# Two chained gated layers behind a linear attention: the last down product of block 0 from halves, blocks 1 and 2 sent out through partial rows in DRAM, and a new order of the first 400 tasks

## The chip, the cores and the metric

One NeuronCore of a Trainium2 chip runs the whole program. The metric is device time in microseconds (us), the median over runs. TensorE (PE in the rows) multiplies, VectorE (DVE) and ScalarE (ACT) do elementwise work, GpSimd (POOL) issues the accumulating transfers and SyncE (SP) all other transfers.

## What is computed

```python
def _attn_ref(q, k, v):                      # batch 2, 8 heads, 768 steps, head size 64
    for t in range(S):
        state = gamma * state + einsum('bhd,bhe->bhde', k[:, :, t], v[:, :, t])
        y[:, :, t] = scale * einsum('bhd,bhde->bhe', q[:, :, t], state)

def _moe_ref(x, w_in, w_out):                # 1536 tokens, 512 -> 2048 -> 512
    h = x @ w_in
    return (h * clip(h + 3, 0, 6) / 6) @ w_out

def _moe2_ref(x, w_in, w_out):               # the same sizes
    h = x @ w_in
    return (h * tanh(log1p(exp(h)))) @ w_out

x = attention output as (1536, 512);  out = _moe2_ref(_moe_ref(x))
```

All in float32. The kernel keeps that precision by splitting each operand of a big product into a high and a low part and multiplying three times (high by high, low by high, high by low).

## The kernel before

The 1536 tokens are three blocks (0, 1, 2) of 512 columns. The 2048 hidden rows are 16 tiles of 128, taken as eight pairs `p`, and the pairs as four groups `g` of two (`NG = 4`, `NP = 2`). In every layer a group first makes its hidden tiles (up products) and then multiplies them by the second weight matrix (down products), so there are eight rounds of up and down, after an attention part.

Blocks 1 and 2 of a pair are, but for one pair of the first group, made together by a scheme with seven products instead of eight (`up_pair`, products `P1` to `P7`, who = "w"; block 0 is done the same way with halves of its own columns, who = "v"). Six matmuls make one product. Its recombination runs through three PSUM tiles X, Z (tags `wx`, `wy`) and Y (`wy`): `s1` copies X to SBUF on ScalarE (L930), product 2 goes into Y, and `c11` adds Y to the copy on VectorE (L933). The activation then reads the sum.

The down products of a group of the second layer are one of three (the first layer has `pair_down` in groups 1 and 2, and direct products else):

- `pair_down` ("p"): blocks 1 and 2 together, seven products `k` in the order 1, 5, 6, 3, 7, 2, 4 of twelve matmuls of 512 columns each.
- `half_down` ("b" of the groups in `HD`, before 1 and 2): block 0 by the same seven products, but on two halves of 256 columns; twelve matmuls of 256 columns to a product. Ahead of each, VectorE forms a difference (`less`, L1204), ScalarE rounds to the high part (L1225) and VectorE makes the low part (L1226).
- `block_down` ("b" of the others): block 0 directly, four tiles by four output rows by three matmuls of 512 columns.

`AFTER` says the order in a group: ("bp", "bp", "bp", "pb"), so the last group does `pair_down` first and block 0 last. What a group adds to the output is copied out of PSUM (`copied`, L1057, ScalarE) and added to partial rows in DRAM (`into_part`: the first write by SP, L1069, the later ones by an accumulating transfer of POOL, L1071). In the last group nothing goes to the partial rows: `read_back` (L1080) brings all of them to SBUF, `into_back` adds the products onto them on VectorE (L1063) and SP stores the sums to the output (L1098).

The order of all work is made when the program is built: each step is a task with an engine, a modelled duration and its dependencies; the first tasks stand in the string `SEQ`, word for word in the order in which they are issued, and the rest is put in order by rank and modelled time (`Plan.order`). Each engine then runs its own tasks strictly in that order, SP's transfers too. In the names of tasks `lq`, `lk` and `w0_` are loads of queries with keys, of values, and of weights; `sc`, `kv`, `qv`, `pv` are the attention products of one of twelve units; `hi`, `lo` make the parts of a hidden tile; `y` is a store to the output. `TOPS` and `KPD` say by a letter which engine (A for ScalarE, D for VectorE) does one conversion of a weight load, or one scaling of values.

Of the kernel before, what the change touches and what calls it, by code (L numbers as in the profile page):

```python
# [70 lines left out]
HD = (1, 2)  # L71
# [4 lines left out]
SEQ = ("ones cst0 lq0 dum0 zero lq1 dum1 tri top0 dum2 rows dum3 lk0 dum4 lk1 warm0 lk2 warm1 lq2 sc0 lq3 lq4 sc1 m0_0 m0_1 tab0 "  # L76
# [18 lines left out]
BORDER = {"pb": (2, 3, 0, 1), "bp": (0, 1, 2, 3)}  # L95
TOPS = "AAAAAAADDADADDAAAAAADDAAAADDAAAA"
KPD = "DDDDDDAAADAA"
# [154 lines left out]
def body(ctx: ExitStack, tc: tile.TileContext, aps: dict, out: bass.AP):  # L252
# [640 lines left out]
    def up_pair(who, layer, p):  # L893
# [10 lines left out]
        n = first.stop  # L904

# [34 lines left out]
        s1 = snap(1, X, first, g11, first, p1)  # L940
        if seq_of(who, layer, p) == EARLY_Y:
            p2 = product(2, Y, True, first, [p1])
            p5 = product(5, Z, True, last, [p2])
        else:
            p5 = product(5, Z, True, last, [p1])
            p2 = product(2, Y, True, first, [p5])
# [415 lines left out]
    for g in range(NG):  # L1362
        for key in flow1[g]:
            need(key)
        if g == NG - 1:
            for b in (1, 2, 0):
                read_back(b)
# [74 lines left out]
```

## Time and profile before

| | |
|---|---|
| runs | median 530.24 us of 3 (529.26 to 533.11) |
| profiled execution, its own time | 528.86 us |
| its span in the trace | 527.1 us |
| TensorE busy | 521.0 us (99%) |
| VectorE busy | 447.2 us (85%) |
| ScalarE busy | 356.0 us (68%) |
| GpSimd busy | 58.0 us (11%) |
| mean granted clock of TensorE | 0.998 of full speed |

The span runs from the first to the last instruction; the profiled execution's own time is 1.76 us more. Matmuls overlap in the trace (one of 512 columns is shown with 390 ns, though the next one starts after about 227 ns), so their pace is read from a run of many, not from the mean of one.

### The profile page before, as it was taken

Reading aid. Unit: us, or ns where it says so; the run is one execution under the profiler, and the core shown is the slowest. Engines: PE = TensorE matmul, PEld = TensorE weight load, DVE = VectorE, ACT = ScalarE, POOL = GpSimd, SP = SyncE. Lnnn points to the kernel's source line nnn. Section 1 sums busy time; section 2 is a strip of 40 time slices with the busy share of each in tenths; the row PEclk is TensorE's granted clock in tenths of the full one; section 3 lists DMA queues with packets and bytes.
Section 4 is the critical chain, followed back from the end, with each engine's and each line's share of the span. In section 5 each row is a group of like instructions: output and inputs, shape, how many; then the busy total and the mean of one; then the engine's idle time right before and its main releaser. Section 6 shows DMA issues by size and latency. Waiting matters only on the chain.

```text
span 527.1 us, 8602 instructions
## 1 busy us (share of the span) xinstructions
PE 521.0 (99%) x3186; PEld 444.7 (84%) x3186; DVE 447.2 (85%) x745; ACT 356.0 (68%) x646; POOL 58.0 (11%) x70
## 2 busy tenths in 40 slices
PE   8999999999999999999999999999999999999996
PEld 5888888888889888888888898888998899888885
DVE  4999998799998969778889999977899879987892
ACT  3488496757786666686655777776768778786540
POOL 1000000001330020340000000020024300540000
PEclk9999999999999999999999999999999999999999
DMA  8995115443994362798530024682149941995532
GB/s 329 406 410 196 29 52 168 159 156 92 175 193 124 134 139 35 147 127 267 195 130 2 0 81 140 220 199 100 63 116 150 241 133 32 183 123 116 188 137 105
DMA packets 27179, 78.92 MB, mean 150 GB/s; under 512 B 3024, under 2 KB 4432, under 8 KB 27136
## 3 DMA queue, kind: packets, MB, share of 16 engines
q1 hardware_dynamic: 17920, 61.58, 32.3%
q0 software_dynamic: 9216, 16.78, 22.1%
q8 instruction: 25, 0.41, 0.3%
q14 instruction: 18, 0.15, 0.1%
HBM read 52.13 MB, written 26.21 MB: 149 GB/s over the span
## 4 chain that ended last, share of the span: by engine, by line
PE 97%; DMA 1%; DVE 1%; issue 0%; DVEq 0%
PE acc L285 50%; PE wx L285 26%; PE wy L285 21%; DMA kv<-in_kv_dram 1%; DVE A L687 0%; DVE vp L680 0%; DVE xch L1063 0%; DVEq L1437 0%; DVE t L494 0%; DVE bias L266 0%; DVEq L680 0%
## 5 line engine op out<-in xcount | busy, mean ns | idle before, releaser
L285 PE MATMUL acc<-gh,wdl 128*128 128x512 f32 (+1 forms) x216 | 82.6, 382 | 0.0
L285 PE MATMUL acc<-gh,wdh 128*128 128x512 f32 (+1 forms) x216 | 82.5, 382 | 0.0
L285 PE MATMUL acc<-gl,wdh 128*128 128x512 f32 (+1 forms) x216 | 82.3, 381 | 0.0
L1071 POOL DMA_DIRECT2D part<-sb x42 | 37.6, 937 | 387.9 <-ACT sb L1057 294.5
L285 PE MATMUL acc<-gh,sb 128*128 128x512 f32 (+1 forms) x204 | 57.1, 365 | 0.0
L285 PEld LDWEIGHTS acc<-gl,wdh 128*128 128x128 f32 x216 | 40.6, 188 | 7.9
L612 DVE TENSOR_TENSOR cv<-cv 128x256 f32<-128x256 f32 x108 | 45.5, 422 | 1.6
L285 PEld LDWEIGHTS acc<-gh,wdh 128*128 128x128 f32 x216 | 40.7, 188 | 7.2
L285 PEld LDWEIGHTS acc<-gh,wdl 128*128 128x128 f32 x216 | 40.7, 188 | 7.1
L979 ACT CAST gh<-g 128x512 fp32r<-128x512 f32 x54 | 33.5, 621 | 18.0 <-PE acc L285 13.7
L981 DVE TENSOR_TENSOR gl<-g,gh 128x512 fp32r<-128x512 f32 x54 | 37.2, 688 | 9.8 <-PE acc L285 4.8
L285 PEld LDWEIGHTS acc<-gh,sb 128*128 128x128 f32 x204 | 36.5, 189 | 5.9
L554 DVE SCALAR_TENSOR_TENSOR cv<-raw,top 128x1024 int32<-128x1024 int32 (+1 forms) x34 | 39.3, 1157 | 0.4 <-ACT top L549 0.2
L285 PE MATMUL acc<-gl,sb 128*128 128x512 f32 (+1 forms) x102 | 37.1, 364 | 0.0
L979 ACT CAST gh<-gs 128x512 fp32r<-128x512 f32 x43 | 26.7, 620 | 14.9 <-PE acc L285 14.1
L1057 ACT ACTIVATE sb<-acc 128x512 f32<-128x512 f32 x52 | 30.9, 600 | 6.5 <-PE acc L285 5.7
L549 ACT ACTIVATE top<-raw 128x1024 f16<-128x1024 bf16 (+1 forms) x25 | 32.1, 1283 | 1.1 <-DMA raw<-in_w_dram 1.1
L981 DVE TENSOR_TENSOR gl<-gs,gh 128x512 fp32r<-128x512 f32 x43 | 29.6, 688 | 3.4 <-ACT gh L979 2.8
L565 DVE SCALAR_TENSOR_TENSOR wdl<-cv,wdh 128x512 fp32r<-128x512 f32 x32 | 21.6, 686 | 7.6 <-ACT wdh L563 7.3
L285 PE MATMUL wy<-xbh,wsh 128*128 128x512 f32 x60 | 23.5, 392 | 0.0
L285 PE MATMUL wy<-xbh,wsl 128*128 128x512 f32 x60 | 23.4, 390 | 0.0
L285 PE MATMUL wx<-q,wsh 128*128 128x512 f32 x60 | 23.3, 389 | 0.0
(252 smaller groups left out, 1459.0 us busy)
## 6 DMA issues: line engine op xcount, KB each, us to landing
raw<-in_w_dram SPq DMA_DIRECT2D x30, 1023.8 KB, 4.8
part<-sb POOLq DMA_DIRECT2D x42, 256.0 KB, 5.0
qk<-in_qk_dram SPq DMA_DIRECT2D x12, 512.0 KB, 7.3
kv<-in_kv_dram SPq DMA_DIRECT2D x10, 516.0 KB, 6.4
part<-sb SPq DMA_DIRECT2D x18, 256.0 KB, 2.1
part<-q POOLq DMA_DIRECT2D x10, 256.0 KB, 4.9
q<-part SPq DMA_DIRECT2D x8, 256.0 KB, 6.1
raw<-in_w_dram SPq DMA_DIRECT2D x4, 511.8 KB, 7.9
```

Of the source, the lines that this page charges most:

```text
L285: nc.tensor.matmul(o, l, r, start=start, stop=stop, skip_group_check=True)
L549: a1 = add(nm + "t", "ACT", act(n) * 1.33, [ld, top_free[0]], [rb, t_b], lambda: A.activation(top(), high(), AF.Copy, scale=0.5))
L554: top_free[0] = add(nm + "o", "DVE", dve(n), [a1], [rb, t_b, cb], lambda: V.scalar_tensor_tensor(out=cb.tile.bitcast(I32)[:, cs], in0=low( ...
L565: return add(nm + "lo", "DVE", dve(n), [a], list(dict.fromkeys([cb, hb, lb])), lambda: V.scalar_tensor_tensor(out=lb.tile[:, l0:l0 + n], i ...
L612: prev = [add(nm + f"s{o}", "DVE", dve(256), prev, [cb], lambda o=o, x=x, y=y, op=op: V.tensor_tensor(out=q(o), in0=q(x), in1=q(y), op=op))]
L979: a = add(f"hi{nm}", "ACT", act(512), deps + [prev_split[0]], [gb, gh], lambda: A.copy(gh.tile, gb.tile))
L981: lambda: V.tensor_tensor(out=gl.tile, in0=gb.tile, in1=f32(gh.tile), op=ALU.subtract))
L1057: lambda: A.activation(tp.tile, ac.tile, AF.Copy, scale=sc), rk)
L1071: landed[tp] = added[layer, b, d] = add(f"pa{nm}", "POOL", ADDED, [dep, added[layer, b, d], *more], [tp, pt], lambda: nc.gpsimd.dma_start( ...
```

## The change

Three edits that can be told apart, and a table.

1. `HD` gets group 3: the last block-0 product is `half_down` in place of `block_down`. Its sums are added onto the rows read back and stored in eight pieces of 256 columns.
2. `pair_down` of the last group no longer uses `into_back`: its products are copied out by ScalarE and accumulated into the partial rows by POOL, as in the other groups, and once a row has had its last addition SP copies it from the partial row to the output, DRAM to DRAM (new, L1196 of the changed kernel). Only block 0's rows are read back (four transfers in place of twelve).
3. `ONTO` lists eight pairs for which `s1` copies X into the PSUM tile Y instead of SBUF; product 2 is then accumulated onto it (no fresh start), the addition `c11` is gone, and the activation reads Y.
4. `SEQ` has another order and more tasks, and `TOPS`, `KPD` change three letters each.

```diff
+ONTO = ((0, 2), (0, 3), (0, 5), (0, 6), (0, 7), (1, 3), (1, 5), (1, 7))
-HD = (1, 2)
+HD = (1, 2, 3)
...
-    "m1_0 otab0 tab1 otab1 tab4 m1_1 tab2 vp0 tab5 tab3 otab5 vp1 kv0 otab3 pv0 lk3 kv1 vp2 pv1 st1 lk4 otab4 lq5 st0 xf1_0 "
+    "otab2 m0_1 tab4 tab0 vp0 tab1 otab0 m1_1 otab1 kv0 pv0 lk3 vp1 tab5 tab3 otab5 vp2 kv1 st0 otab4 pv1 lk4 otab3 lq5 kv2 "
...
-TOPS = "AAAAAAADDADADDAAAAAADDAAAADDAAAA"
-KPD = "DDDDDDAAADAA"
+TOPS = "AAAAADDADADADDAAAAAADDAAAADDAAAA"
+KPD = "DDDDAAADADAA"
...
+        early = seq_of(who, layer, p) == EARLY_Y
+        onto = who == "w" and not early and ((layer, p) in ONTO)
...
-        s1 = snap(1, X, first, g11, first, p1)
+        s1 = snap(1, X, first, Y if onto else g11, first, p1)
...
-            p2 = product(2, Y, True, first, [p5])
+            p2 = product(2, Y, not onto, first, [p5] + ([s1] if onto else []))
...
-        c11 = plus(11, Y, first, g11, first, [p2, s1])
+        c11 = p2 if onto else plus(11, Y, first, g11, first, [p2, s1])
...
-            gval[layer, f, 1] = (g11, [mish_or_swish(f"{layer}_{f}_1", layer, g11, [c11])])
+            gval[layer, f, 1] = (g11, [mish_or_swish(f"{layer}_{f}_1", layer, g11, [c11], src=Y if onto else None)])
...
-                if final:
-                    into_back(nm, ac, b, dd, [last[d]], rk, k in (3, 7, 2, 4))
-                    ev[banks[k][d]] = back[b, dd][1] if k not in (3, 7, 2, 4) else []
-                elif k == 3:
+                if k == 3:
...
+                if layer and g == NG - 1 and k in (3, 7, 2, 4):
+                    pt = part[1, b, dd]
+                    add(f"y{nm}", "SP", 0.8, [added[1, b, dd]], [pt], lambda b=b, dd=dd, pt=pt: nc.sync.dma_start(
+                        out=out[dd * P:(dd + 1) * P, b * TB:(b + 1) * TB], in_=pt.tile))
...
-            for b in (1, 2, 0):
-                read_back(b)
+            read_back(0)
```

On SP, at the very end of the program, this stands before; `xal`, `xah` and `xch` are the rows of blocks 2, 1 and 0 in SBUF:

```order
L1098 DMA out_dram<-xal_5152 128x512 x4
L1098 DMA out_dram<-xah_5149 128x512 x4
L1098 DMA out_dram<-xch_5243 128x512 x3
L1098 DMA out_dram<-xch_5243 128x256 x2
L1437 UNCONDITIONAL_BRANCH
```

and this after the change; `part_337` to `part_340` are block 1's partial rows, `part_341` to `part_344` block 2's:

```order
L1196 DMA out_dram<-part_341_3614 128x512
L1196 DMA out_dram<-part_342_3621 128x512
L1196 DMA out_dram<-part_343_3546 128x512
L1279 DMA out_dram<-xch_5232 128x256 x2
L1196 DMA out_dram<-part_337_3514 128x512
L1279 DMA out_dram<-xch_5232 128x256 x4
L1196 DMA out_dram<-part_344_3554 128x512
L1279 DMA out_dram<-xch_5232 128x256 x2
L1196 DMA out_dram<-part_338_3524 128x512
L1196 DMA out_dram<-part_339_3694 128x512
L1196 DMA out_dram<-part_340_3698 128x512
L1445 UNCONDITIONAL_BRANCH
```

The stores of block 0 were the last of the queue; now three copies of partial rows stand behind the last two of them.

On TensorE block 0 came last before, tile by tile; near its end stood

```order
L285 MATMUL acc_987_5417<-wbl_995_5441,wdh_5091 128x512
L285 MATMUL acc_984_5424<-wbh_994_5436,wdh_5091 128x512
L285 MATMUL acc_984_5424<-wbh_994_5436,wdl_5103 128x512
L285 MATMUL acc_984_5424<-wbl_995_5441,wdh_5091 128x512
L285 MATMUL acc_985_5429<-wbh_994_5436,wdh_5091 128x256
```

and now, as far from the end, stands the seventh half product, whose matmuls read `wbh_1000` and `wbl_1001`, the parts that ScalarE and VectorE make:

```order
L288 MATMUL acc_997_5531<-gl_5502,wdh_5084 128x256
L288 MATMUL acc_982_5409<-wbh_1000_5519,wdh_4984 128x256
L288 MATMUL acc_982_5409<-wbh_1000_5519,wdl_4994 128x256
L288 MATMUL acc_982_5409<-wbl_1001_5535,wdh_4984 128x256
L288 MATMUL acc_983_5422<-wbh_1000_5519,wdh_4984 128x256
```

All 84 matmuls behind the last pair product have 256 columns, where 45 of 512 and 6 of 256 stood.

On SP near the start, the eleventh to sixteenth transfer (`kv` values, `qk` queries with keys, `raw` weights) stood before as

```order
L315 DMA kv_177<-in_kv_dram 128x1032
L315 DMA kv_199<-in_kv_dram 128x1032
L303 DMA qk_219<-in_qk_dram 128x1024
L534 DMA raw_237<-in_w_dram 128x2047
L315 DMA kv_261<-in_kv_dram 128x1032
```

and now as

```order
L318 DMA kv_171<-in_kv_dram 128x1032
L318 DMA kv_193<-in_kv_dram 128x1032
L306 DMA qk_217<-in_qk_dram 128x1024
L318 DMA kv_237<-in_kv_dram 128x1032
L537 DMA raw_258<-in_w_dram 128x2047
```

The first three, and all ahead of them, keep their places; the weights are one place later.

## Rows read from the trace of the kernel before

**Rows 1.** The page's first part: busy time, share and instructions of each engine
```profile
span 527.1 us, 8602 instructions
PE 521.0 (99%) x3186; PEld 444.7 (84%) x3186; DVE 447.2 (85%) x745; ACT 356.0 (68%) x646; POOL 58.0 (11%) x70
```

**Rows 2.** Busy time by stretch; last columns: granted clock, DMA share, GB/s
```profile
core 0: us, PE busy (x) PEld busy (x) DVE busy (x) ACT busy (x) POOL busy (x), PEclk, DMA share, GB/s
4.32:20.00 15.68, 15.08 (x255) 12.62 (x256) 11.26 (x18) 5.87 (x13) 0.00 (x0) 1.00 1.01 392
...
20.00:60.00 40.00, 39.89 (x540) 34.25 (x537) 38.06 (x64) 28.74 (x76) 0.00 (x0) 1.00 0.68 264
...
500.00:520.00 20.00, 20.00 (x90) 16.57 (x89) 13.84 (x23) 6.53 (x11) 0.00 (x0) 1.00 0.29 107
```

**Rows 3.** All that TensorE waited for: us in total, times, longest
```profile
PE acc L285 <- DVE t L494: 1.2, 1, 1.2
PE acc L285 <- DVE vp L680: 0.3, 1, 0.3
PE wy L285 <- DVE A L687: 0.2, 1, 0.2
```

**Rows 4.** The chain that ended last, from 10 us: start, us, what
```profile
10.30 6.43 DMA kv<-in_kv_dram
...
17.57 2.03 PE acc L285 x48
```

**Rows 5.** The same chain later: runs of down products and one up product
```profile
390.28 1.39 PE wx L285 x6
391.67 19.04 PE acc L285 x84
...
436.62 5.03 PE acc L285 x42
...
495.05 27.95 PE acc L285 x126
```

**Rows 6.** Line 930, the copies out of PSUM: ns min/median/max, first and last start
```profile
L930 ACT COPY gs<-wx x15: 569/587/590, 82.7 to 483.2; 128x512 f32<-128x512 f32 x15
```

**Rows 7.** VectorE in order of time during a half product: start, us, what
```profile
435.65 0.42 DVE L1204 TENSOR_TENSOR wsl<-wsl 128x256 f32<-128x256 f32 x1
435.99 0.42 DVE L1204 TENSOR_TENSOR wsh<-wsh 128x256 f32<-128x256 f32 x1
...
438.33 0.42 DVE L1226 TENSOR_TENSOR wbl<-wsl,wbh 128x256 fp32r<-128x256 f32 x1
...
439.74 0.42 DVE L1226 TENSOR_TENSOR gl<-wsl,gh 128x256 fp32r<-128x256 f32 x1 [0.15 <-ACT gh L1225]
```

**Rows 8.** All engines in order of time: the pair product's last split, and the end
```profile
508.46 0.69 DVE L981 TENSOR_TENSOR gl<-gs,gh 128x512 fp32r<-128x512 f32 x1 [0.23 <-PE acc L285]
...
522.71 0.28 PE L285 MATMUL acc<-wbl,wdh 128*128 128x256 f32 x1
...
523.02 0.76 DVE L1063 TENSOR_TENSOR xch<-acc,xch 128x256 f32<-128x256 f32 x2
523.03 1.33 SPq L1098 DMA_DIRECT2D out_dram<-xch  x3
```

**Rows 9.** SP's issues in order of time: three in a row
```profile
493.60 1.37 SPq L1080 DMA_DIRECT2D xch<-part  x3
```

**Rows 10.** Transfers from 520 us on: KB each, median us from issue to landing
```profile
out_dram<-xch SPq DMA_DIRECT2D x3, 256.0 KB, 2.4
out_dram<-xch SPq DMA_DIRECT2D x2, 128.0 KB, 2.1
```

**Rows 11.** SP's twelve reads of partial rows, 484 to 495 us
```profile
DMA to landing us min/median/max: 2.6/3.9/5.0
```

**Rows 12.** The page's DMA issues: reads of the first layer's partial rows
```profile
q<-part SPq DMA_DIRECT2D x8, 256.0 KB, 6.1
```

**Rows 13.** POOL's accumulating transfers of the third group, 440 to 480 us
```profile
DMA to landing us min/median/max: 3.8/4.7/6.5
```

**Rows 14.** The page's groups: issue of an accumulating transfer, copy out of PSUM
```profile
L1071 POOL DMA_DIRECT2D part<-sb x42 | 37.6, 937 | 387.9 <-ACT sb L1057 294.5
L1057 ACT ACTIVATE sb<-acc 128x512 f32<-128x512 f32 x52 | 30.9, 600 | 6.5 <-PE acc L285 5.7
```

More of the change, by code (lines that the diff above doesn't have):

```diff
@@ L75 @@
 AFTER = ("bp", "bp", "bp", "pb")
-SEQ = ("ones cst0 lq0 dum0 zero lq1 dum1 tri top0 dum2 rows dum3 lk0 dum4 lk1 warm0 lk2 warm1 lq2 sc0 lq3 lq4 sc1 m0_0 m0_1 tab0 "
[18 rows of a table removed]
+SEQ = ("ones cst0 lq0 dum0 zero lq1 dum1 tri top0 dum2 rows dum3 lk0 dum4 lk1 warm1 lk2 warm0 lq2 sc0 lq3 lq4 sc1 m0_0 tab2 m1_0 "
[20 rows of a table added]
 BORDER = {"pb": (2, 3, 0, 1), "bp": (0, 1, 2, 3)}
-TOPS = "AAAAAAADDADADDAAAAAADDAAAADDAAAA"
-KPD = "DDDDDDAAADAA"
+TOPS = "AAAAADDADADADDAAAAAADDAAAADDAAAA"
+KPD = "DDDDAAADADAA"
 def dve(n, two=True):
@@ L939, in up_pair @@
         p1 = product(1, X, True, first, ahead)
-        s1 = snap(1, X, first, g11, first, p1)
-        if seq_of(who, layer, p) == EARLY_Y:
+        s1 = snap(1, X, first, Y if onto else g11, first, p1)
+        if early:
             p2 = product(2, Y, True, first, [p1])
@@ L1036, in body, with spare @@
     spares, landed = {}, {}
-    def copied(layer, nm, ac, dep, rk):
+    def spare(layer):
         if layer not in spares:
@@ L1046, in copied @@
             spares[layer] = own
+    def copied(layer, nm, ac, dep, rk):
+        spare(layer)
         tp = spares[layer][taken[0] % len(spares[layer])]
@@ L1074, in read_back @@
     def read_back(b):
-        whole = buf("fix", [P, 2048], ("xch", "xah", "xal")[b])
+        whole = buf("fix", [P, 2048], "xch")
         for d in range(4):
@@ L1104, in pair_down @@
         ps = range(g * NP, (g + 1) * NP)
-        final = layer == 1 and g == NG - 1
         pd, z = ("pd", "") if layer else ("pd0", "0")
@@ L1230, in form @@
             return gh, gl, low
+        spare(1)
         free = sum([tform[1, w][n][2] for w in "wv" for n in ("T1", "T2", "T3", "T4")], [])
```

36 rows, old and new, of the table SEQ are left out of this document.

## The prediction

> **What bounds the kernel now.** I read the busy times first [rows 1]: TensorE is busy 521.0 of 527.1 us, VectorE 447.2, ScalarE 356.0. Busy is not yet bound, so next come the stretches [rows 2]: from 20 us on TensorE has no idle time worth naming (39.89 of the 40 us to 60, then 20.00 of 20 up to 520), with the full clock granted. Then its waits [rows 3]: three in the whole program, 1.7 us, of which 1.2 stand before its first matmul. The chain that ended last confirms it: behind 17.57 us it is nearly all TensorE [rows 4, 5]. So three things can move the time: the amount of TensorE's work; its start, which hangs on loads; and what comes after its last matmul. Elsewhere a saved instruction buys nothing unless TensorE then has less to do, and an added one costs nothing until TensorE or the last store waits for it.
>
> **The pace of a matmul.** In the chain 84 matmuls of 512 columns take 19.04 us, 0.2267 each; 42 of 256 columns in a half product take 5.03 us, 0.1198 each [rows 5]. A half therefore costs 53% of a whole. Those two divisions price the main edit.
>
> **Block 0 of the last group from halves.** Removed: 45 × 0.2267 + 6 × 0.1198 = 10.92 us. Added: 7 products × 12 matmuls × 0.1198 = 10.06 us. TensorE gains 0.86 us, on the path that sets the end. The Trainium skill (TensorE: Matmul & The Clock Gate, section "Back-to-back issue gap") states for a warm matmul by itself a gap of N / 2.4 + 2.5 ns, 216 ns for 512 columns and 109 for 256; by it this gain would be 1.2 us and the sum below +1.0. The rows show the longer gaps for this kernel's products [rows 5], so the measured ones decide.
>
> What the halves need from the others: the old block-0 product wanted four splits, the new one wants 14 low parts, 8 differences and 14 additions on VectorE, 36 instructions of 256 columns. Back to back they start 0.335 us apart (435.65 to 438.33 is eight intervals) though each is shown with 0.42 [rows 7]. The last full-width split of the pair product started at 508.46 and ends at 509.15 [rows 8]; in the changed kernel VectorE no longer has the additions onto read-back rows there, so it can start then. The 32 instructions up to the last low part take 32 × 0.335 = 10.7 us, to 519.9. TensorE ends the pair product near 512.1 (its present end, 523.0, less 10.92), and reaches the last six matmuls 9.3 us later, at 521.4. The cover is 1.5 us. If every instruction had to wait out its full 0.42 us, VectorE would be ready at 522.6, 1.2 us late. I take 0.3 us for small stalls, nearer to the covered end because the halves of groups 1 and 2 ran without a wait of TensorE [rows 3, 5]; ends 0 and 1.2.
>
> **Blocks 1 and 2 through partial rows.** Twelve reads and eight stores from SBUF go; twelve copies on ScalarE, twelve accumulating transfers (two more VectorE additions, for product 3, stay) and eight DRAM-to-DRAM copies come. Fourteen VectorE additions of 0.68 us leave a stretch where ScalarE is busy 6.53 us of 20 [rows 2], so twelve copies of 0.60 us [rows 14] fit there: 0. The accumulations: the last pair product ends near 512.1; two copies take it to 513.4, two issues of 0.94 us [rows 14] to 515.3, landing 4.7 us after issue at the median and 6.5 at most [rows 13], so about 519 to 521. The final stores come at 523 to 524; they cover this by 2 us or more, and I cost it at 0.
>
> What is not covered is SP's queue. Before, the last store of block 0 was the last transfer. Now three copies of partial rows are issued behind it, though their data have landed by then, and SP issues strictly in order. Each issue takes 0.46 us (three in 1.37) [rows 9], so the last transfer starts 1.37 us later than before. Then its landing: a store from SBUF lands 2.1 us after issue (128 KB, the last kind) and 2.4 (256 KB) [rows 10]. No row shows DRAM to DRAM; the nearest are SP's reads of partial rows, 2.6 us at the quickest, 3.9 at the median in a burst [rows 11], and 6.1 in the busy first layer [rows 12]. Against 2.1 that is +0.5, +1.8 or +4.0. I take +0.5, since at the end the queue is short, as it was for the first of the reads. From below: the copies could land as quickly as a store, +0. The tail costs 1.37 + 0.5 = 1.9 us; ends 1.4 and 5.4.
>
> **Product 2 accumulated onto a copy in PSUM.** Eight additions of VectorE go, on an engine that TensorE waits for 0.5 us in all [rows 3]: 0 gained. A wait is added: product 2 now waits for ScalarE's copy, and all of TensorE's queue stands behind it. The copy takes 0.587 us [rows 6]; between product 1 and product 2 stands at least product 5, six matmuls of 512 columns, 1.39 us [rows 5], so 0.8 us are to spare even where nothing else is put between. No row shows ScalarE writing PSUM, so from both sides: a copy that costs nothing gains nothing (TensorE does not wait); one that is wholly exposed costs eight times 0.587, 4.7 us. I take 0, the side of the 1.39 us.
>
> **The new order of the first 400 tasks.** From 4.32 to 20 us the DMA share is 1.01 at 392 GB/s [rows 2]: loads, not the order on TensorE, set the pace. The chain shows where: the values of unit 3 are awaited until 16.73, and TensorE is solid from 17.57 [rows 4]. That load and everything ahead of it keep their places in SP's queue, so 17.57 should stay. What is idle after it and before 60 us is some 0.4 us [rows 2, 3]; that is the most to gain. The loss has a size too: one load pushed behind another costs 512 KB at 392 GB/s, 1.3 us. I take 0; ends −0.4 and +1.3. The letters of the two tables move conversions between two engines with idle time: 0.
>
> **Sum.** −0.86 (TensorE) + 0.3 (stalls) + 0 + 0 + 0 (loads) + 1.9 (tail) = +1.3 us, on the profiled execution's own 528.86: 530.2. That execution lies 1.4 us below the median of the runs, 530.24, so the median forecast is 531.5. A measurement of this kernel can tell about 1% (5.3 us) from no change, and this is a quarter of it.
>
> **Rivals.**
> - *The tail hides itself.* If the three copies overlap with what follows a store anyway and the stalls are none, −0.86 − 0.4 + 1.4 is about 0: 530.3. For it: the data of the copies are ready 2 us before. Against: the order of SP is fixed, and an issue takes its 0.46 us. Chance 0.2; within 1%.
> - *The copies from DRAM are slow.* At the 6.1 us of the first layer's reads the tail costs 5.4, and the sum is −0.86 + 0.3 + 5.4 = +4.8: 535.1. For it: source and target are both DRAM, eight copies beside eight stores. Against: transfers are few at the end, and stores land in 2.1 to 2.4 us. Chance 0.1; mostly within 1%, a third of it beyond.
> - *VectorE becomes the bound of the last product.* Each difference is followed by ScalarE's rounding and VectorE's low part, and strict order makes VectorE wait in between: a row shows 0.15 us of such idle time on top of 0.42 [rows 7]. If each of the 32 instructions took 0.57 us, the last low part would come at 509.15 + 18.2 = 527.4, 6 us after TensorE wants it: −0.86 + 6 + 1.9 = +7.0, 537.3, slower by over 1%. It decides from a mean pace of 1.5 / 32 = 0.05 us above 0.335, that is from 0.38. For it: 86% of VectorE's time there would be taken. Against: two pairs alternate, so one's rounding lies beside the other's low part, and groups 1 and 2 show 0.335. Chance 0.04.
> - *The start gains much, or TensorE's waits go.* All waits that could go are 0.5 us [rows 3], too little for 1%. Chance 0.02, for what the trace does not show.
>
> **How the numbers follow.** The forecast has 0.64, the hiding tail 0.2, slow copies 0.1, VectorE 0.04, a gain unseen 0.02. Faster by over 1%: 0.02. Slower: 0.04 and a third of slow copies, 0.07. Within 1%: 0.91. The range leaves out the VectorE case and the worst of the slow copies; at its lower end it takes the hidden tail, 530.3, less 1.3 us because the three runs before lie 1.0 below and 2.9 above their median: 529.0. At its upper end it takes half of the way from the forecast to slow copies and 1 us of the same scatter: 534.3.
>
> **What would show it.** Right: from 20 us on TensorE stays without idle time; the stretch behind the last pair product is near 10.1 us where it was 10.9; the chain ends with SP's copies from partial rows, not with block 0's stores; the last transfer starts about 1.4 us after block 0's last store; the solid part of TensorE begins near 17.6. Wrong: idle time of TensorE before matmuls that read the parts of the half products (then VectorE is the bound), waits of TensorE on line 930's copies or on loads before 60 us, an accumulation that lands after 523 us, or a chain that still ends with block 0.

## The result, and the profile after

The changed kernel takes 534.04 us at the median of ten runs (532.88 to 535.08), the kernel before 529.33 beside it: a ratio of 1.0084, interval 1.0069 to 1.0100. That is 4.7 us slower where 1.3 were forecast; 534.04 lies in the range of 529.0 to 534.3, close to its upper end. The direction, and "within 1%", were right; the size was not. The number 531.5 is missed by 2.5 us and the change by 3.4, because the forecast started from a median of 530.24 and the kernel before now has 529.33. The profiled execution took 533.87 us, 5.0 more than that of before.

The page of the changed kernel, its first part and its DMA queues (packets, MB, share of 16 engines' span):

```profile
span 532.1 us, 8732 instructions
...
PE 520.3 (98%) x3219; PEld 445.3 (84%) x3219; DVE 443.4 (83%) x752; ACT 364.5 (69%) x675; POOL 68.7 (13%) x82
...
q1 hardware_dynamic: 17200, 59.48, 31.7%
q0 software_dynamic: 10944, 19.93, 26.2%
```

and the same line of GpSimd's queue in the page of the kernel before:

```profile
q0 software_dynamic: 9216, 16.78, 22.1%
```

TensorE is busy 0.7 us less than in [rows 1], and the span is 5.0 us longer: the time is not in TensorE's work. It has 12 accumulating transfers more (1728 packets, 144 each), and their queue takes 26.2% of 532.1, 139.4 us of all sixteen engines, where it took 22.1% of 527.1, 116.5. So the packets of one accumulation of 256 KB take as long as 22.9 / 12 = 1.9 us of all sixteen engines. The page of before already said so: 116.5 us over its 64 accumulations is 1.8 each.

The chain that ended last, at the start and at the end (start, us, what). TensorE's solid part begins at 17.86, where 17.57 stands in [rows 4], and 0.63 us of idle time without a visible cause follow at 30.05:

```profile
17.86 1.56 PE acc L288 x32
...
30.05 0.63 issue
```

```profile
495.96 17.03 PE acc L288 x75
...
513.00 10.06 PE acc L288 x81
...
523.08 0.78 DVE xch L1274 x2
```

SP's issues at the end, in order of time; L1279 are block 0's stores, L1196 the copies from partial rows:

```profile
519.16 1.12 SPq L1279 DMA_DIRECT2D out_dram<-xch  x2
520.33 1.34 SPq L1196 DMA_DIRECT2D out_dram<-part  x1
521.76 2.03 SPq L1279 DMA_DIRECT2D out_dram<-xch  x4
523.89 0.50 SPq L1196 DMA_DIRECT2D out_dram<-part  x1
524.48 1.03 SPq L1279 DMA_DIRECT2D out_dram<-xch  x2
525.61 2.08 SPq L1196 DMA_DIRECT2D out_dram<-part  x3
```

With [rows 1, 5, 8] these rows divide the 5.0 us of span without a rest:

| piece | before | after | change | forecast |
|---|---|---|---|---|
| start of the last run of down products | 495.05 | 495.96 | +0.91 | 0 (−0.4 to +1.3) |
| from there to the end of the last matmul | 27.95 | 17.03 + 0.01 + 10.06 = 27.10 | −0.85 | −0.86 + 0.3 |
| last matmul's end to the end of block 0's last store issue | 524.36 − 523.00 = 1.36 | 525.51 − 523.06 = 2.45 | +1.09 | 0 |
| copies issued behind it | 0 | 527.69 − 525.51 = 2.18 | +2.18 | +1.37 |
| last issue to the end of the span | 527.1 − 524.36 = 2.74 | 532.1 − 527.69 = 4.41 | +1.67 | +0.5 |

The last three lines, the tail, are +4.94 where +1.9 was forecast. The other two nearly cancel. How busy the transfer engines were behind it (columns as in [rows 2]; the last but one is the DMA share):

```profile
495.00:510.00 15.00, 15.00 (x70) 12.56 (x70) 9.24 (x14) 11.35 (x21) 6.10 (x7) 1.00 0.90 160
510.00:519.00 9.00, 8.99 (x63) 8.11 (x62) 8.17 (x24) 5.85 (x16) 4.20 (x5) 1.00 1.10 229
519.00:526.00 7.00, 4.40 (x37) 4.20 (x35) 4.67 (x14) 0.81 (x2) 0.17 (x1) 1.00 1.01 233
526.00:532.00 6.00, 0.00 (x0) 0.00 (x0) 0.00 (x0) 0.00 (x0) 0.00 (x0) 0.70 0.63 203
```

In [rows 2] the share from 500 to 520 us was 0.29. Now it is 0.90 to 1.10 from 495 to 526: the engines are crowded when the last stores are issued. (The share adds up the time of packets, and 1.10 shows that these can overlap; it is read here as a measure of crowding.) And this is when each kind lands (KB each, median us from issue to landing, from 519 us on), against 2.4 and 2.1 us in [rows 10]:

```profile
out_dram<-part SPq DMA_DIRECT2D x5, 256.0 KB, 4.0
out_dram<-xch SPq DMA_DIRECT2D x8, 128.0 KB, 3.2
part<-sb POOLq DMA_DIRECT2D x1, 256.0 KB, 4.9
```

The accumulation in this list is the last one. Its issue, from GpSimd's instructions in order of time:

```profile
518.28 0.88 POOL L1079 DMA_DIRECT2D part<-sb  x1 [1.41 <-issue]
```

It lands 4.9 us later, at 523.2, where the prediction said 519 to 521 and named a landing after 523 as a sign of being wrong.

TensorE's waits, which answer to [rows 3]:

```profile
PE acc L288 <- DVE t L497: 1.2, 1, 1.2
PE acc L288 <- DVE vp L683: 0.8, 2, 0.6
PE acc L288 <- issue: 0.6, 1, 0.6
PE wy L288 <- DVE A L690: 0.5, 1, 0.5
```

All lie in the first 60 us; none is at a half product, and none at the copies into PSUM.

### The profile page after: what moved, and what is told of

Same layout as the page of the kernel before. It is cut to its first block, busy times and chain, and to the rows that moved or that the text cites. A ratio compares the mean times of both kernels' runs of the same rounds, so it can differ in the third digit from the quotient of the medians.

```text
span 532.1 us, 8732 instructions
## 1 busy us (share of the span) xinstructions
PE 520.3 (98%) x3219; PEld 445.3 (84%) x3219; DVE 443.4 (83%) x752; ACT 364.5 (69%) x675; POOL 68.7 (13%) x82
## 3 DMA queue, kind: packets, MB, share of 16 engines
q0 software_dynamic: 10944, 19.93, 26.2%
## 4 chain that ended last, share of the span: by engine, by line
PE 96%; DMA 1%; DVE 1%; issue 0%; DVEq 0%
PE acc L288 50%; PE wx L288 25%; PE wy L288 21%; DMA kv<-in_kv_dram 1%; DVE vp L683 0%; DVE A L690 0%; DVE xch L1274 0%; DVE t L497 0%; DVE bias L269 0%; DVEq L683 0%
## 5 line engine op out<-in xcount | busy, mean ns | idle before, releaser
L1079 POOL DMA_DIRECT2D part<-sb x50 | 44.5, 933 | 415.8 <-ACT sb L1065 317.5
L288 PE MATMUL acc<-gh,wdh 128*128 128x512 f32 (+1 forms) x212 | 80.8, 381 | 0.0
L288 PE MATMUL acc<-gh,wdl 128*128 128x512 f32 (+1 forms) x212 | 80.7, 381 | 0.0
L288 PE MATMUL acc<-gl,wdh 128*128 128x512 f32 (+1 forms) x212 | 80.5, 379 | 0.0
L288 PE MATMUL acc<-gh,sb 128*128 128x512 f32 (+1 forms) x228 | 61.6, 356 | 0.0
L288 PEld LDWEIGHTS acc<-gh,sb 128*128 128x128 f32 x228 | 40.3, 189 | 5.9
L1065 ACT ACTIVATE sb<-acc 128x512 f32<-128x512 f32 x60 | 35.7, 599 | 9.3 <-PE acc L288 8.6
L288 PE MATMUL acc<-gl,sb 128*128 128x512 f32 (+1 forms) x114 | 40.6, 356 | 0.0
L566 ACT ACTIVATE wdh<-cv 128x512 fp32r<-128x512 f32 x32 | 19.9, 630 | 10.0 <-DVE cv L557 6.9
L288 PEld LDWEIGHTS acc<-gl,sb 128*128 128x128 f32 x114 | 21.6, 189 | 3.1
```

The lines of the kernel that those rows point to most:

```text
L288: nc.tensor.matmul(o, l, r, start=start, stop=stop, skip_group_check=True)
L566: lambda: A.activation(hb.tile[:, h0:h0 + n], cb.tile[:, c0:c0 + n], AF.Copy, scale=256.0))
L1065: lambda: A.activation(tp.tile, ac.tile, AF.Copy, scale=sc), rk)
L1079: landed[tp] = added[layer, b, d] = add(f"pa{nm}", "POOL", ADDED, [dep, added[layer, b, d], *more], [tp, pt], lambda: nc.gpsimd.dma_start( ...
```

## Experiments

Two suspects stood at the outset, the front (the new order) and the tail; then two explanations of the tail. The letters of the theories are those of each set of runs, and each text says what its theory holds. "Behind the last matmul" is the span less the end of the chain's last run of matmuls: 527.1 − 523.0 = 4.1 in the kernel before, 532.1 − 523.06 = 9.0 in the changed one. It is read from one execution of each kernel; the first run below has the same tail as the changed kernel and 532.0 − 523.66 = 8.3, so differences of 0.7 us are not read as effects. Each ratio is to the kernel before on the same chip.

### Which part of the change costs the time

**Changed kernel, old order.**

```diff
-SEQ, TOPS, KPD of the changed kernel
+SEQ, TOPS, KPD of the kernel before
```

> The changed kernel with the old task order and the old letters of the two tables; the other three edits stay. Theory N (the new order costs time by itself: the load of unit 7's values is issued 3.5 us later than before because product kv4, which releases its buffer, was moved behind sc5 and qv5, and TensorE waits in the first 35 us): TensorE's first up product starts near 33.0 us instead of 34.0, and the time falls by about 1.0 us, to 533.0. Rival R1 (the late start is scatter of the loads between executions): no change, 534.0.

Measured: 533.9 us, ratio 1.0089 (1.0073 to 1.0104). The loss is whole without the new order, as the rival said.

**Changed kernel, old tail.** Blocks 1 and 2 of the last group by `into_back` again, with twelve reads and VectorE's fourteen additions; halves, copies into PSUM and new order stay.

```diff
-            read_back(0)
+            for b in (1, 2, 0):
+                read_back(b)
...
+                if final:
+                    into_back(nm, ac, b, dd, [last[d]], rk, k in (3, 7, 2, 4))
...
-                if layer and g == NG - 1 and k in (3, 7, 2, 4):
-                    pt = part[1, b, dd]
```

> The changed kernel with blocks 1 and 2 of the last group added onto rows read back and stored from SBUF, as before; halves, copies into PSUM and new order stay. Theory N (the tail is lost to the transfer engines, which the twelve accumulations and eight copies fill from 507 to 530 us): the last store lands about 3 us after the last matmul again, and the time is the kernel before plus 1.0 (order) minus 0.7 (halves), 529.7. Rival R2 (the halves themselves, by VectorE or by eight stores of 256 columns, make the tail long): at least 532.

Measured: 529.33 us, ratio 1.0002 (0.9993 to 1.0011); 3.7 us behind the last matmul. The partial rows and their copies are the loss, all of it.

**Kernel before with halves and copies into PSUM.**

```diff
-HD = (1, 2)
+ONTO = ((0, 2), (0, 3), (0, 5), (0, 6), (0, 7), (1, 3), (1, 5), (1, 7))
+HD = (1, 2, 3)
...
```

> The kernel before with two edits alone: block 0 of the last group from halves, and the eight products accumulated onto a copy in PSUM; old order, old way of blocks 1 and 2. Theory N: TensorE does 0.86 us less and stalls 0.2, so 0.6 us faster than before, 528.7. Rival R2: VectorE, which now does fourteen additions more in the stretch ahead, holds the half products up: 1 us slower or more. Rival R3 (the accumulated products make TensorE wait): idle time of TensorE before the second products, slower by 0.5 us or more.

Measured: 529.38 us, ratio 1.0014 (0.9994 to 1.0033). TensorE has 0.86 us less to do and the time does not fall; it does not rise by 1 us either, as the rival R2 had it. The chain of this run, and VectorE's last low part in it, say why:

```profile
511.99 0.70 DVE xah L1069
...
512.83 10.92 PE acc L286 x81
...
523.78 0.78 DVE xch L1272 x2
```

```profile
522.63 0.41 DVE L1232 TENSOR_TENSOR wbl<-wsl,wbh 128x256 fp32r<-128x256 f32 x1
```

The half products, 10.06 us in the changed kernel, take 10.92 here, just what they were to save, and the chain enters them by way of VectorE's addition onto `xah`. From that addition on VectorE has no idle time, and its last low part starts 9.80 us after the first half product; in the changed kernel it starts 521.83 − 513.00 = 8.83 after. This kernel keeps the fourteen additions; the changed one has moved them away. The halves need that relief.

**Kernel before with the new order alone.**

```diff
-SEQ, TOPS, KPD of the kernel before
+SEQ, TOPS, KPD of the changed kernel
```

> The kernel before with the new task order and the new letters alone. Theory N: the first up product starts 1.0 us later and the time is 1.0 us above before, 530.3. Rival R1: no change.

Measured: 530.61 us, ratio 1.0026 (1.0014 to 1.0037), with its last run of down products from 495.88 as in the changed kernel (495.96). Alone the order seems to cost 1.4 us; taken out of the changed kernel it gave nothing back. The two runs before this one are a third pair that differs in the order alone, on the same chip: 529.33 us with the new one, 529.38 with the old.

**Kernel before with the copies into PSUM alone.**

```diff
+ONTO = ((0, 2), (0, 3), (0, 5), (0, 6), (0, 7), (1, 3), (1, 5), (1, 7))
...
```

> The kernel before with only the eight second products of layer pairs summed by TensorE onto the copy in PSUM instead of by a VectorE addition. All theories: 0, that is 528.9 to 529.9 us, ratio 0.999 to 1.001; over 530.2 would say that this edit hid a loss in the changed kernel.

Measured: 529.36 us, ratio 0.9998 (0.9988 to 1.0008): nothing, as forecast.

### What in the tail costs it

**Last four copies on ScalarE's queue.**

```diff
-                    add(f"y{nm}", "SP", 0.8, [added[1, b, dd]], [pt], lambda b=b, dd=dd, pt=pt: nc.sync.dma_start(
+                    late = k in (2, 4)
+                    t = add(f"y{nm}", "ACT" if late else "SP", 0.1 if late else 0.8, [added[1, b, dd]], [pt],
+                            lambda b=b, dd=dd, pt=pt, late=late: (nc.scalar if late else nc.sync).dma_start(
...
+    for t in outs:
+        t.after = prev_split[0]
```

> The changed kernel, with the last four copies from the partial rows to the output (those of products 2 and 4) issued on ScalarE's queue behind its last cast, so that block 0's eight stores no longer stand behind a copy that waits. Theory N (the engines that move the data have no time left: 12 accumulations of 1.8 to 1.9 us of all of them each, eight copies and eight stores between 496 and 531): the same bytes have to be moved, the end comes 0 to 2 us sooner, 532 to 534 us. Rival S (SP's queue: a waiting copy and 0.6 us an issue hold block 0's stores up): the last store of block 0 lands some 3.5 us sooner and the end with it, about 530.5 us.

Measured: 533.36 us, ratio 1.0076 (1.0060 to 1.0093). SP's queue was not cleared, though. One copy is left between block 0's stores, and now it waits, by the profile for a copy of the other queue to land:

```profile
SPq L1198 <- DMA out_dram<-part: 1.7, 1, 1.7
```

So this run does not settle the point by itself.

**Plain writes instead of accumulations.** The output's blocks 1 and 2 hold only last addends.

```diff
-                out=pt.tile, in_=tp.tile, accum_op=ALU.add))
+                out=pt.tile, in_=tp.tile, **({} if nm[0] == "3" else {"accum_op": ALU.add})))
```

> The changed kernel, with the last group's twelve transfers of blocks 1 and 2 to the partial rows as plain writes instead of accumulating ones; the output's rows of blocks 1 and 2 then hold only the last addend of each row. The same number of transfers, waits and issues. Theory N: a plain write of 256 KB takes under half the time of an accumulating one, so 12 times about 1 us of engine time goes; the transfers before the last store land on time and only the three copies behind it are left, 530 to 531.5 us. Rival S: the issues on SP stand where they stood, 533 to 533.5 us.

Measured: 534.72 us, ratio 1.0095 (1.0074 to 1.0115). The rows show the engines relieved and the end unmoved (stretches; then the last matmuls in the chain; then SP's issues; then the landing of all eight copies, and of the three from 526 us on):

```profile
510.00:519.00 9.00, 8.99 (x59) 7.96 (x59) 7.94 (x22) 5.93 (x16) 2.70 (x5) 1.00 0.78 254
519.00:526.00 7.00, 5.25 (x44) 5.04 (x43) 5.51 (x16) 1.29 (x4) 0.00 (x0) 1.00 0.52 161
```

```profile
513.85 10.06 PE acc L288 x81
```

```profile
524.96 1.01 SPq L1279 DMA_DIRECT2D out_dram<-xch  x2
526.08 2.09 SPq L1196 DMA_DIRECT2D out_dram<-part  x3
```

```profile
DMA to landing us min/median/max: 3.0/3.3/4.0
DMA to landing us min/median/max: 3.4/3.7/4.0
```

The theory of full engines falls as the only cause: the share drops from 1.01 to 0.52, and still three copies stand behind the last store for 2.09 us of issues and land 3.4 to 4.0 us later. It is 8.6 us behind the last matmul, and the three pieces of the tail are those of the changed kernel: 525.97 − 523.91 = 2.06 to the end of block 0's last store issue, 528.17 − 525.97 = 2.20 for the copies, 532.5 − 528.17 = 4.33 to the end, against 2.45, 2.18 and 4.41. How slow a copy from DRAM to DRAM is by itself shows in the one issued at 521.18, between the stores: it lands after 3.0 us with the share at 0.42 (519 to 524), 0.6 more than the 2.4 of a store of the same size in [rows 10]. The last three come close together, with the share at 0.77 from 524 to 531, and land later one after the other.

**Without the eight copies.** Blocks 1 and 2 of the output are not written.

```diff
-                if layer and g == NG - 1 and k in (3, 7, 2, 4):
-                    pt = part[1, b, dd]
...
```

> The changed kernel without the eight copies from the partial rows to the output: blocks 1 and 2 of the output are not written; the twelve accumulations stay. Theory N: the accumulations alone (23 us of all engines over 27 us) are done by 523, and block 0's stores after that end as in the kernel before: 529 to 530 us. Were the accumulations alone too much for the engines, block 0's last store would land over 1 us later than in the kernel before and the time be over 530.5 us. Rival S: about 529.

Measured: 528.27 us, ratio 0.9979 (0.9966 to 0.9992), 3.6 us behind the last matmul. The twelve accumulations alone cost nothing, and the rest of the change then gains 1.1 us. The copies are the loss.

**The last copies from SBUF.** Block 1 of the output is only its last addend.

```diff
-                    add(f"y{nm}", "SP", 0.8, [added[1, b, dd]], [pt], lambda b=b, dd=dd, pt=pt: nc.sync.dma_start(
+                    add(f"y{nm}", "SP", 0.8, [added[1, b, dd]], [pt, tp], lambda b=b, dd=dd, pt=(pt if k in (3, 7) else tp): nc.sync.dma_start(
```

> The changed kernel with the last four of the eight copies (rows 338 to 340 and 337 of the partial rows) taken from the SBUF tile that holds the last addend instead of the row in DRAM, so that block 1 of the output is only its last addend; same places in SP's queue, same number. Q: the order's 2.0 us of issues stay, the landing after the last issue falls from 4.0 to about 2.1 us, as a store's: 531.8 to 532.3 us. If the landing is late only because the engines are busy with what was issued ahead: 533.3 to 534.

Measured: 533.4 us, ratio 1.0067 (1.0050 to 1.0084). The median lies in the second range; the ratio, on the 529.33 of the result, gives 532.9, between the two. It is not told apart from the changed kernel's 1.0084. Its profiled execution started late, so only its end is read: 8.3 us behind the last matmul. From 519 us on the four transfers took:

```profile
out_dram<-sb SPq DMA_DIRECT2D x4, 256.0 KB, 3.5
```

A store from SBUF that should land in 2.1 to 2.4 us takes 3.5 when the engines are crowded (their share was 1.00 from 526 to 532 us). The changed kernel's copies took 4.0, so the source in DRAM seems the smaller part of the late landing.

**The last four copies on GpSimd's queue**, behind the last accumulation.

```diff
-add(f"y{nm}", "SP", 0.8, ..., nc.sync.dma_start(
+add(f"y{nm}", "POOL" if k in (2, 4) else "SP", 0.8, ..., (nc.gpsimd if k in (2, 4) else nc.sync).dma_start(
```

> The changed kernel with the same four copies issued on GpSimd's queue behind the last accumulation, in place of SP's. Q: SP's last store is issued as in the kernel before but for one copy among them; the copies go out as their accumulations land, the last at about 523.5 to 524.5, and lands 4 us later, 527.5 to 528.5, so 529.5 to 531 us. If landing on the loaded engines sets the end wherever the copies are issued: 532.5 to 533.5.

Measured: 533.83 us, ratio 1.0083 (1.0070 to 1.0096). This time nothing stands behind block 0's last store on SP: its issue is the last one, and ends at 526.15, though one copy (0.50 us from 524.06) is still issued just ahead of the last two stores. But look at GpSimd's last copy, the landing and the share:

```profile
524.65 1.50 SPq L1279 DMA_DIRECT2D out_dram<-xch  x2
524.27 0.53 POOL L1196 DMA_DIRECT2D out_dram<-part  x1 [0.90 <-DMA part<-sb]
```

```profile
out_dram<-part POOLq DMA_DIRECT2D x4, 256.0 KB, 5.3
out_dram<-xch SPq DMA_DIRECT2D x8, 128.0 KB, 5.1
```

```profile
519.00:526.00 7.00, 4.93 (x42) 4.72 (x40) 5.19 (x15) 0.98 (x3) 2.97 (x5) 1.00 1.04 238
526.00:532.00 6.00, 0.00 (x0) 0.00 (x0) 0.00 (x0) 0.00 (x0) 0.00 (x0) 0.77 0.61 226
```

Block 0's small stores, 2.1 us in [rows 10], land 5.1 after issue, and GpSimd's copies cannot go out sooner, at 519.53 the first and at 524.27 the last: they stand behind the last accumulation, and two of them wait, by the profile for accumulations to land. What was taken from SP's queue comes back as later landing; it is 8.2 us behind the last matmul. The Trainium skill says as much (DMA: Bandwidth & Descriptors, section "Issuing engines are not separate DMA queues"): whichever engine issues, the transfers run on the same sixteen engines, and only issue time is saved. This trace agrees: their share is 1.04 from 519 to 526 us, and the time is the changed kernel's.

**Both edits together**: plain writes, and the copies on GpSimd's queue.

```diff
+**({} if nm[0] == "3" else {"accum_op": ALU.add})
...
+(nc.gpsimd if k in (2, 4) else nc.sync).dma_start(
```

> Both edits that failed alone put together: the last group's twelve transfers to the partial rows as plain writes (the output's blocks 1 and 2 then hold only last addends), and the last four copies on GpSimd's queue. Theory T (two limits end at nearly the same time: the transfer engines, which the accumulations fill until about 523 and the copies overfill by 8 times 0.7 us; and SP's order, in which three copies of 3 to 4 us stand behind the last store; taking away one leaves the other): with both gone the end falls to a store's landing after the last matmul, 529 to 530.5 us. Theory Q' (each copy from DRAM lands late by itself, wherever it is issued and whatever the engines do): 532.5 to 533.5, as either alone.

Measured: 530.79 us, ratio 1.0023 (1.0012 to 1.0034); 5.4 us behind the last matmul. It lies 0.3 us above what theory T gave and 1.7 below the rival's numbers. Each edit alone gave nothing, the two together about 3.3 us (534.04 to 530.79; by the ratios 0.6%). This is the mark of two limits side by side (landing of the stores, and GpSimd's last copy):

```profile
out_dram<-xch SPq DMA_DIRECT2D x8, 128.0 KB, 2.3
519.69 0.52 POOL L1196 DMA_DIRECT2D out_dram<-part  x1 [1.58 <-DMA part<-sb]
```

The stores are back at 2.3 us, and GpSimd's copies go out from 515.79 to 519.69, some 4 us sooner than with accumulations, because the plain writes are issued and land sooner. Of the 1.3 us that remain against the 4.1 of before, 0.7 stand ahead of the end of block 0's last store issue (525.99, 2.06 behind the last matmul where it was 1.36), with one copy still among these stores; 0.6 stand behind it (529.3 − 525.99 = 3.3 where it was 2.74).

### Versions that keep the gain

**Block 1 by VectorE, block 2 by partial rows.**

```diff
-                if final:
+                if final and b == 1:
                     into_back(nm, ac, b, dd, [last[d]], rk, k in (3, 7, 2, 4))
...
-                if layer and g == NG - 1 and k in (3, 7, 2, 4):
+                if final and k in (3, 7):
...
```

> The changed kernel with block 1 of the last group (products 1, 2 and 4, the last two of which end latest) summed on VectorE onto rows read back, as in the kernel before, and only block 2 by way of the partial rows and copies: six accumulations and four copies instead of twelve and eight. Theory N: some 11 us of accumulating instead of 23, all issued before 516, so that the engines are free again when block 0's last stores are issued: 529 to 530 us; if VectorE's eight additions fewer let the half products run at their pace, down to 528.5. Rival S: the waiting copies of block 2 stand ahead of block 0's first stores, not its last: also 529 to 530, so this run asks only whether a shorter tail can be had with VectorE relieved.

Measured: 530.0 us, ratio 1.0011 (1.0000 to 1.0022); 4.0 us behind the last matmul. Six accumulations and four early copies cost nothing at the end, but six additions onto `xah` suffice to hold up the half products, which take 10.92 us again.

**Partial rows in the output.** Layer 2's partial rows of blocks 1 and 2 are the output's own rows, so that nothing has to be copied.

```diff
+    for b in range(1, NBLK):
+        for d in range(4):
+            part[1, b, d].make = lambda b=b, d=d: out[d * P:(d + 1) * P, b * TB:(b + 1) * TB]
...
-                if layer and g == NG - 1 and k in (3, 7, 2, 4):
-                    pt = part[1, b, dd]
```

> The changed kernel without the eight copies because layer 2's partial rows of blocks 1 and 2 are kept in the output's own rows: the first write and the accumulations go straight there. The same number of writes and accumulations, the reference's output. Theory Q (the loss is the copies: three of them stand last in SP's queue, 2.0 us of issues, and a copy from DRAM to DRAM lands 4.0 us after its issue where a store lands 2.1 after its own; the accumulations cost nothing): as the run that left the copies out, last landing 2.6 us after the last matmul's start, 528 to 528.8 us, ratio 0.997 to 0.999. Theory N (the engines that move data are full of the accumulations): has fallen with the run of plain writes, it would give 531.

Measured: 528.9 us, ratio 0.9991 (0.9976 to 1.0006). SP's end and the engines:

```profile
519.73 5.23 SPq L1278 DMA_DIRECT2D out_dram<-xch  x8
```

```profile
510.00:519.00 9.00, 8.99 (x60) 8.04 (x59) 8.15 (x23) 6.02 (x16) 4.36 (x5) 1.00 1.01 150
519.00:526.00 7.00, 4.97 (x42) 4.77 (x40) 5.24 (x16) 1.02 (x3) 0.00 (x0) 1.00 0.86 217
```

Eight stores and nothing behind them; the engines are crowded until 519 us and less so from then on: 3.6 us behind the last matmul.

**The same with the old order.**

```diff
-SEQ, TOPS, KPD of the changed kernel
+SEQ, TOPS, KPD of the kernel before
```

> The version that keeps the partial rows in the output's own rows, with the kernel before's order of the first 400 tasks. If the order costs what it cost alone on the kernel before (1.0026): 527.5 to 528; if nothing, as the version with the new order: 528.5 to 529.2.

Measured: 528.37 us, ratio 0.9988 (0.9978 to 0.9999): the fastest kernel here that leaves no work out, between the two forecasts. It beats the changed one by about 1%, and the one before by a tenth of a per cent, at the edge of what its interval excludes.

**The same with the new order and without the halves.**

```diff
-HD = (1, 2, 3)
+HD = (1, 2)
```

> The same version (new order, partial rows in the output's rows) without the halves: the last group's block 0 takes its second products over whole columns again. The prediction's term for the halves, with VectorE relieved of its fourteen additions: 0.86 us off TensorE less 0.3 of stalls, so this run is 0.5 to 0.6 us slower than with halves, 529.3 to 529.7; if the halves are worth nothing in the changed kernel either, 528.7 to 529.1.

Measured: 530.07 us, ratio 1.0013 (1.0005 to 1.0022), above both forecasts; its last run of down products is 27.95 us again, where the version with halves has 27.10. With halves the ratio was 0.9991, so they are worth some 0.2%, 1.2 us, by intervals that just touch; the rows alone show 0.85.

## Why the prediction was wrong in size, point by point

**The step that failed is the tail**: "The tail costs 1.37 + 0.5 = 1.9 us". It measured 4.94. The order of events was as forecast, SP's three copies behind block 0's last store; each part was too small. Three issues took 2.18 us, not 1.37. From the last issue to the end it took 1.67 more than before, not 0.5 "since at the end the queue is short": a copy by itself would have cost about that (3.0 us against a store's 2.4), but three come one behind the other and behind the last stores. And block 0's own last store went out 1.09 us later, which had no term, because two copies stand among the stores; one of their issues took 1.34 us, which is scatter (0.50 in the run with the old order, where the store went out 0.7 later than before).

**The accumulations' crowding does not make these three pieces**: with plain writes they are 2.06, 2.20 and 4.33. They come from SP's order and from copies that land late in each other's company. Behind them lies a second limit, which the prediction also left out: the sum of the transfers. I gave the accumulations 0 because they would land in time. By themselves they do cost nothing: without copies the end is 3.6 us behind the last matmul, less than the 4.1 of before, though in the version with its rows in the output the last of them lands at 523.4. But the page before had their price of 1.8 us of all sixteen engines each: 22.9 us for twelve, to be fitted in from 496 us on, beside eight copies. In shares, 0.90 × 15 + 1.10 × 9 + 1.01 × 7 + 0.63 × 6 = 34.2 us of work in 37 in the changed kernel. So with SP's queue cleared behind the last store (copies on GpSimd's) the copies wait for accumulations that land late, and the end stays; with the engines relieved (plain writes) SP's order holds it; with both gone it falls by about 3.3 us. That the landing of the accumulations and the crowding are one limit and not two is argued from these rows; no run parts them.

**The rival of slow copies** named +4.8 and 535.1; the execution shows +5.0. Its number was nearly right by luck, and its mechanism a part of it: copies from DRAM land 3.0 us after issue alone and up to 4.0 as three in a row, not 6.1, four stores from SBUF in their place took 3.5, and SP's order supplies the rest. That 534.04 lies in the range is luck of the same kind: its upper end was drawn halfway to this rival. I had given it 0.1, on the argument that "transfers are few at the end".

**Halves**: −0.86 forecast with 0.3 of stalls, −0.85 measured with no wait on record. But the cover was not the 1.5 us I worked out. VectorE began the halves at 510.55, not at 509.15: 0.91 us of this is the later start of the whole stretch, the rest a wait for ScalarE's rounding. These rows show its first low part and its last:

```profile
510.55 0.43 DVE L1234 TENSOR_TENSOR wbl<-wsh,wbh 128x256 fp32r<-128x256 f32 x1 [0.48 <-ACT wbh L1233]
...
521.83 0.42 DVE L1234 TENSOR_TENSOR wbl<-wsl,wbh 128x256 fp32r<-128x256 f32 x1
522.16 0.75 DVE L1274 TENSOR_TENSOR xch<-acc,xch 128x256 f32<-128x256 f32 x2
```

It ends at 522.25, and the last run ends with six matmuls of 0.12 us each before 523.06, so 0.1 us was to spare. The rival in which VectorE holds the halves up was near; the three runs that keep additions of blocks 1 and 2, or of block 1 alone, on VectorE show it, with the whole gain lost.

**Product 2 onto the copy in PSUM**: 0 forecast, ratio 0.9998 measured alone. **The new order**: 0 forecast, with ends −0.4 and +1.3. The profiled execution starts its last run 0.91 us later than before, TensorE being busy 39.37 of the 40 us to 60 (39.89 in [rows 2]):

```profile
20.00:60.00 40.00, 39.37 (x548) 33.97 (x545) 37.18 (x63) 30.57 (x80) 0.00 (x0) 1.00 0.71 265
```

Whether that is the order stays open. Alone it cost 1.4 us, beyond its interval; by the ratios it cost −0.3 us in the changed kernel, 0.2 in the version with its rows in the output, and −0.6 in the kernel with halves and the old tail, none beyond the intervals. And this start differs from execution to execution under one order: with the old one it lies between 495.05 and 496.57 in five kernels, with the new one between 495.09 and 496.83 in eleven, and at 499.38 in the one that started late.

## What to carry to other kernels

Before adding transfers to the last stretch, look at what an issuing queue that runs in order has behind the last store: three copies there cost some 4 us, with the transfer engines crowded or not. Then add up what the transfers hold: the queue's share of the page times the span over its transfers gives engine time for each kind, and what the last ones wait for must have landed before. Where an edit that removes a suspected limit changes nothing, remove two at once before giving the suspect up: the limits may stand side by side. And a row that is summed in DRAM only to be copied to the output can be summed in the output, if nothing else writes there.

## What the runs showed of the hardware

- The packets of an accumulating transfer of 256 KB take 1.9 us of the sixteen engines, those of a plain one in its place 0.7: with plain writes the line of GpSimd's queue, which was 139.4 us in the changed kernel, is 23.4% of 532.5, 124.6 us, 14.8 us less for twelve.

```profile
q0 software_dynamic: 10176, 19.93, 23.4%
```

- A copy of 256 KB from DRAM to DRAM lands 3.0 us after issue alone between stores (share 0.42), up to 4.0 as the last of three in a row (share 0.77), and at a median of 5.3 with the share at 1.04; a store of 128 KB goes from 2.1 us to 5.1.
- Half products take 10.06 or 10.92 us for the same matmuls, with no wait above 0.2 us on record: VectorE's pace shows in the length of a run of matmuls sooner than in the waits.
